# A retention and feed-forward kernel: each piece's outputs and the next piece's scores issued together

## The chip, the cores and the metric

One core of one Trainium2 chip runs the whole program. The metric is the device time in microseconds (us). Engines are named as in the profile: PE is TensorE's matmul, PEld its weight load (which overlaps matmuls), DVE is VectorE, ACT is ScalarE, POOL is GpSimd, SP is SyncE. SP does no arithmetic here; it issues nearly all DMA transfers, one after the other, from one queue.

## What is computed

A retention layer (8 batches, 8 heads, 576 positions, 64 dimensions a head), whose result is bridged to 4608 rows of 512 and fed through a feed-forward layer with 2048 hidden units:

```python
scores = scale * np.matmul(q, k.transpose(0, 1, 3, 2))
Dmat = np.where(rel >= 0, gamma[:, None, None] ** rel[None, :, :], 0.0)
attn_out = np.matmul(scores * Dmat[None], v)
x = attn_out.transpose(0, 2, 1, 3).reshape(4608, 512)
h = x @ w_in                                            # 512 x 2048
sp = np.maximum(h, 0.0) + np.log1p(np.exp(-np.abs(h)))
out = (h * erf(sp)) @ w_out                             # 2048 x 512
```

All inputs and outputs are float32; the weights arrive as 64-bit words and are rounded on the chip.

## The kernel before, in words

**Retention, by pieces.** The 4608 rows are cut into 36 pieces of 128 rows, numbered 0 to 35. Every ninth piece (8, 17, 26, 35) holds two half pieces of 64 rows, the tails of two batches. Retention runs in chunks within a batch: a piece needs its own scores and a running state that the piece before it left. A piece goes through three stages:

- `transposes(i)`, called T(i) below: queries and keys are brought into transposed form. For queries from piece 8 on and keys from piece 12 on this is done by DVE (L326) out of tiles `raw_qs` and `raw_ks`, which the DMA delivered in 32-row squares; for earlier pieces by TensorE (L332) and ACT. At its end T(i) calls `load(i + 2, "q")`, which puts the loads of the queries, and from piece 12 on of the keys, of piece i+2 into SP's queue (L131, four issues each for a full piece, eight for a pair of half pieces). `raw_qs` and `raw_ks` have two buffers each, so that load has to wait until T(i) has read its own.
- `scores(i)`, S(i): sixteen weight loads and matmuls on TensorE (L347) into two PSUM banks, then two DVE multiplications by a mask into `sT` (L352, seen as L99 in the profile, the line of the helper `tt`).
- `outputs(i)`, O(i): TensorE multiplies `sT` by the values (L365), adds keys times values for the state (L377) and the old state times the queries (L388); DVE then makes `sums` and two parts of `x` from it, POOL the new state (L426). At its end O(i) calls `load(i + 3, "kv")` (L147) and has POOL weigh the next piece's values (L313).

The list `stages` has them in the order T(i+1), O(i), S(i+1), for i from 0 on. `done[0]` is how many have been issued, and `attend(upto)` issues stages until `upto`. DVE, ACT, POOL and SP each carry out their instructions in the order in which the program issues them.

**Feed-forward, by products.** The rows are also cut into 9 chunks of 512 (four pieces each), the hidden units into 4 groups; the 36 pairs (group, chunk) are the blocks. Each of the two matrix products of a block is done in seven products in place of eight, with sums of sub-matrices, by the classes `First` and `Second`. One product is eight matmuls of 128x256 on TensorE in the profile (L496 for `First`, L604 for `Second`), some 1.7 us. In the order of issue within a block they are

`B11 B21 S4 A22 T2 T3 T1 A11 A12 B22 T4 S2 S3 S1`

where B and T belong to `Second` of a block and A and S (S1 to S4) to `First` of the next blocks. (S with a number of 5 or more, and S in general in the text, is the stage `scores`; products are named S1 to S4 only in this list and where a text says so.) Products accumulate in four PSUM banks: two that alternate (`ps_a`), one named e and one named g (`ps_e`, one buffer each). ACT copies the first partial results away, DVE adds the others: after A22 DVE adds bank g to `t` (`t<-g` in the profile), after which bank g is free for T3; T4's result is added to `o` (`o<-g`), after which g is free for S3. The first two chunks of group 0 are done as plain products (L550).

**How the two are woven.** `run(steps)` goes through a generator of products, and after each product calls `attend` for one more stage; the middle part of `Second` does the same in its own loop. So while pieces remain, TensorE sees three products for each piece, and between them T, O and S, one behind each product. `most[0]` bars the stages of chunks that may not begin yet, and is raised block by block; where the next block needs a chunk that is not finished, `attend(after_chunk(n + 2))` issues what is missing at once. The prologue has an order written out by hand (L754), with stages "a", products "p" and others. All pieces are finished about a third of the way through; the rest are products alone.

The weights are rounded in steps (`round_weights`: ACT L254 and L255, DVE L259, L263, L267, L272, POOL L274 and L275), and in the first third these steps stand between the stages too. Other DMA traffic in SP's queue: `xd<-x` stores a chunk of x for the later groups (L465, 1 MB), `od<-o` stores sums of outputs (L709, 512 KB each), `wraw` loads weights (L237).

Of the kernel before, what the change touches and what calls it, by code (L numbers as in the profile page):

```python
# [54 lines left out]
def kernel(  # L55
# [176 lines left out]
    def load_weights():  # L232
        part = next(coming, None)
        if part is not None:
            t = wraw.tile([P, 2 * WP], UINT32, tag="wraw", name="wraw")
            for rows, src in part[0]:
                nc.sync.dma_start(out=t[rows].rearrange("p (h f) -> p h f", h=2), in_=src)  # L237
            words.append((t, *part[1:]))
# [49 lines left out]
    def round_weights(n=1):  # L288
        for _ in range(n):
            next(round_step, None)  # L290
# [143 lines left out]
    stages = [(transposes, 0), (scores, 0)]  # L434
# [4 lines left out]
    stages = [(of, i) for of, i in stages if i < len(pieces)]  # L439
    done = [0]  # L440

    def before_chunk(c):

        return stages.index((outputs, c * PC)) if c < n_ch else len(stages)

    def after_chunk(c):

        return stages.index((outputs, (c + 1) * PC - 1)) + 1

    def attend(upto):  # L450
        while done[0] < min(upto, len(stages)):
            of, i = stages[done[0]]
            of(i)
            done[0] += 1
# [5 lines left out]
    def load_x(g, c):  # L460
        x[g, c] = x_tile()
        nc.sync.dma_start(out=x[g, c][:, :n_dc], in_=xd[c])
# [6 lines left out]
    def operands_x(g, c):  # L469
        summed.add((g, c))  # L470
        t = x[g, c]
        b11, b12, b21, b22 = (t[:, 2 * d : 2 * d + 2, h * TH : (h + 1) * TH] for d in range(2) for h in range(2))
        t1, t2, t4 = (t[:, n_dc + j, :].rearrange("p (d i) -> p d i", d=2) for j in range(3))
        if g == 0 or c < PLAIN:
            tt(t1, b12, b11, ALU.subtract)
            tt(t2, b22, t1, ALU.subtract)
            tt(b12, b22, b12, ALU.subtract)
        else:
            tt(t2, b12, b11, ALU.add)
            tt(t1, b22, t2, ALU.subtract)  # L480
        if g == 0:
            store_x(c)
        tt(t4, b21, t2, ALU.subtract)
        x[g, c] = {A11: b11, A12: b21, S4: b22, A22: t4, S1: t1, S2: t2, S3: b12}
# [254 lines left out]

    most = [before_chunk(2)]  # L740

    def run(steps, rounds=(), stages=1):

        for step, _ in enumerate(steps):
            attend(min(done[0] + stages, most[0]))
            round_weights(rounds[step] if step < len(rounds) else 0)

    keep_busy(10)
# [5 lines left out]
    for what in "alkakakawkakakawwaa3awa2aaa5ppppaa5wwppa5ppawappwcppa5ppaaapp5s":  # L754
        if what == "a":
            attend(done[0] + 1)
        elif what == "p":
            next(products)
        elif what == "s":
            store_x(0)  # L760
        elif what == "l":
            load(2, "kv")
        elif what == "c":
            nc.sync.dma_start(out=cst[:, CONST_FIRST:], in_=consts[:, CONST_FIRST:])
        elif what == "w":
            load_weights()
        elif what == "k":
            keep_busy(2)
        else:
            round_weights(int(what))  # L770
    most[0] = before_chunk(3)
    attend(after_chunk(1))
    store_x(1)
    for step, _ in enumerate(firsts[1].plain()):
# [8 lines left out]
        elif step == 8:  # L783
            firsts[0].sums()
    seconds[0].begin()
    run(seconds[0].first(), (2, 2))
    firsts[1].softplus()
    most[0] = before_chunk(4)
    for b, nxt in zip(blocks[2:], blocks[3:] + [None]):
        n = order.index((b.g, b.c))  # L790
        if isinstance(b, First):
            most_g[0] = order[n - 1][0] + 1
            run(b.middle(), (1, 1) if n != 2 else ())
            firsts[n - 1].sums()
            run(seconds[n - 1].first(), (1, 1) if n > 2 else ())
            run(b.last(), (1,) if 2 < n < n_ch else ())
            if n in (2, 3):
                load_weights()
            most[0] = before_chunk(n + 3)
        elif n + 2 < n_s:  # L800
            f = firsts[n + 1]
            for step, _ in enumerate(b.middle()):
                attend(min(done[0] + 1, most[0]))
                if step == 0:
                    f.erf()
                elif step == 1 and (n + 2 >= n_ch or done[0] == len(stages)):
                    operands_x(*order[n + 2])
                elif step == 2 and n_ch - 4 < n < n_ch:
                    round_weights()
            if order[n + 2] not in summed:  # L810
                attend(after_chunk(n + 2))
                operands_x(*order[n + 2])
            run(nxt.first(), (1,) if n > 1 else ())
            f.multiply()
            seconds[n + 1].begin()
            if n_ch <= n + 3 < n_s:
                load_x(*order[n + 3])
            run(b.last(), (0, 1) if n > 1 else ())
        elif n + 1 < n_s:
            firsts[n + 1].erf()  # L820
            seconds[n + 1].begin()
            rest = b.rest()
            for _ in range(3):
                next(rest)
            firsts[n + 1].multiply()
            run(rest)
            firsts[n + 1].sums((0,))
            steps = nxt.final()
            next(steps)
            firsts[n + 1].sums((1,))  # L830
            next(steps)
        else:
            run(steps)
# [30 lines left out]
```

## Time and profile before

Four runs gave 1025.52, 1026.39, 1026.18 and 1025.04 us, median 1025.85.

| what | value |
|---|---|
| profiled execution: its time | 1025.52 us |
| its span, first to last instruction | 1023.7 us |
| granted clock of TensorE | 1.00 throughout |
| DVE busy | 668.0 us of the span |
| ACT busy | 390.0 us |
| POOL busy | 122.1 us |
| DMA | 165.76 MB, mean 162 GB/s |
| share of the 16 DMA engines taken by SP's queue | 56.6% |
| first product of a block (L604) | at 83.8 us |
| last retention stage on TensorE (O35) | 311.6 to 313.4 us |

The time by 40 slices shows the two parts: the DMA engines are near full in the first twelve slices (25.6 us each), and half full afterwards; DVE is busier in the first part too. How to read what follows: a line in order of time has the start in us from the first instruction, the busy time in us, the engine, the line of the program, the operation, out<-in, the shape, how many instructions were merged, and in brackets the idle time of that engine just before, with what ended it. "issue" there means that nothing the profile shows was waited for. A stretch (from:to) has the busy time and number of instructions of PE, PEld, DVE, ACT and POOL, the granted clock, the share of the DMA engines that was busy, and GB/s.

### The profile page before, as it was taken

How to read it: one execution, taken by the hardware profiler on the slowest of the kernel's cores; microseconds unless marked ns; L12 is line 12 of the kernel's file. 1: busy time of each engine (PE TensorE's matmuls, PEld its weight loads, DVE VectorE, ACT ScalarE, POOL GpSimd, SP SyncE). 2: the span in 40 equal slices, each digit the busy share in tenths (PEclk: the TensorE clock that was granted, in tenths of full speed). 3: DMA queues.
4: the chain of work that ended last, by engine and by line, in shares of the span. 5: the costliest groups of instructions: out<-in, count | busy, mean ns of one | idle time of the engine just before them, and what ended most of it. 6: DMA issues, size and time to landing. Idle time of an engine off the chain costs nothing.

```text
span 1023.7 us, 15955 instructions
## 1 busy us (share of the span) xinstructions
PE 1014.6 (99%) x6348; PEld 878.3 (86%) x6348; DVE 668.0 (65%) x1062; ACT 390.0 (38%) x481; POOL 122.1 (12%) x122
## 2 busy tenths in 40 slices
PE   9999999999999999999999999999999999999998
PEld 8778888888788888888888888888888888888887
DVE  3769777967976656656666666666567655555555
ACT  2254133234135444334343444444433333333332
POOL 2143112122312010010001001000100000000000
PEclk9999999999999999999999999999999999999999
DMA  9998989979984354544445345434433333444434
GB/s 198 200 234 185 232 192 230 252 152 253 240 190 166 106 163 145 164 158 155 164 139 167 124 147 163 164 144 144 144 124 124 124 131 126 132 136 131 126 85 121
DMA packets 146986, 165.76 MB, mean 162 GB/s; under 512 B 97376, under 2 KB 121568, under 8 KB 138848
## 3 DMA queue, kind: packets, MB, share of 16 engines
q1 hardware_dynamic: 144832, 163.57, 56.6%
q10 hardware_dynamic: 2080, 1.18, 0.5%
q8 instruction: 50, 0.82, 0.3%
q14 instruction: 24, 0.20, 0.1%
HBM read 117.52 MB, written 47.19 MB: 161 GB/s over the span
## 4 chain that ended last, share of the span: by engine, by line
PE 89%; DMA 6%; SPq 2%; DVE 2%; issue 1%; POOL 0%; ACT 0%; ACTq 0%; DVEq 0%; POOLq 0%
PE a L604 23%; PE a L496 22%; PE g L496 11%; PE g L604 11%; PE e L604 6%; PE e L496 5%; PE o L365 3%; PE s L347 2%; DMA raw_v<-in_v_dram 2%; DMA raw_k<-in_k_dram 1%; DMA raw_ks<-in_k_dram 1%; PE o L388 1%; SPq L147 1%; PE o L377 1%; PE p L550 1%; PE f L668 1%
## 5 line engine op out<-in xcount | busy, mean ns | idle before, releaser
L496 PE MATMUL a<-x,wa 128*128 128x256 f32 x1088 | 258.3, 380 | 0.0
L496 PEld LDWEIGHTS a<-x,wa 128*128 128x128 f32 x1088 | 206.1, 190 | 28.6 <-issue 0.7
L604 PE MATMUL a<-wb,s 128*128 128x256 f32 x840 | 200.1, 381 | 0.0
L604 PEld LDWEIGHTS a<-wb,s 128*128 128x128 f32 x840 | 158.6, 190 | 23.0 <-ACT o L618 0.7
L99 DVE TENSOR_TENSOR t<-g,t 128x512 f32<-128x512 f32 x68 | 47.0, 691 | 150.2 <-ACT t L526 112.7
L496 PE MATMUL g<-x,wa 128*128 128x256 f32 x544 | 129.3, 381 | 0.0
L496 PEld LDWEIGHTS g<-x,wa 128*128 128x128 f32 x544 | 102.9, 190 | 14.4 <-issue 0.2
L99 DVE TENSOR_TENSOR o<-a,o 128x512 f32<-128x512 f32 x104 | 71.6, 688 | 46.4 <-PE a L604 46.4
L521 ACT COPY t<-a 128x512 f32<-128x512 f32 x34 | 19.9, 586 | 188.1 <-PE a L496 188.1
L99 DVE TENSOR_TENSOR t<-t,s 128x1024 f32<-128x1024 f32 x72 | 88.6, 1272 | 0.0
L565 ACT ACTIVATE s<-t 128x1024 f32<-128x1024 f32 x72 | 72.1, 1048 | 27.9 <-DVE t L99 27.9
L274 POOL TENSOR_TENSOR wraw<-wraw 128x512 f32<-128x512 f32 x28 | 29.4, 1051 | 436.5 <-DVE wraw L272 184.6
L99 DVE TENSOR_TENSOR x<-x 128x512 f32<-128x512 f32 x115 | 75.7, 692 | 1.2
L532 ACT COPY t<-a 128x512 f32<-128x512 f32 x34 | 19.9, 586 | 144.0 <-PE a L496 144.0
L569 ACT ACTIVATE s<-s 128x1024 f32<-128x1024 f32 x72 | 72.1, 1048 | 0.4
L604 PE MATMUL g<-wb,s 128*128 128x256 f32 x280 | 66.7, 381 | 0.0
L604 PE MATMUL a<-wb,t 128*128 128x256 f32 x280 | 66.6, 381 | 0.0
L604 PE MATMUL e<-wb,t 128*128 128x256 f32 x280 | 66.6, 381 | 0.0
L604 PE MATMUL g<-wb,t 128*128 128x256 f32 x280 | 66.4, 380 | 0.0
L496 PE MATMUL e<-x,wa 128*128 128x256 f32 x272 | 64.8, 381 | 0.0
L99 DVE TENSOR_TENSOR sT<-s,cst 128x512 f32<-128x512 f32 x72 | 46.2, 682 | 25.7 <-PE s L347 25.6
L99 DVE TENSOR_TENSOR o<-g,o 128x512 f32<-128x512 f32 x70 | 48.0, 685 | 21.4 <-ACT o L618 18.7
(86 smaller groups left out, 1248.5 us busy)
## 6 DMA issues: line engine op xcount, KB each, us to landing
od<-o SPq DMA_DIRECT2D x54, 512.0 KB, 3.3
x<-xd SPq DMA_DIRECT2D x27, 1024.0 KB, 4.8
o<-od SPq DMA_DIRECT2D x27, 1024.0 KB, 5.7
raw_qs<-in_q_dram SPq DMA_DIRECT2D x96, 112.0 KB, 4.5
raw_ks<-in_k_dram SPq DMA_DIRECT2D x84, 112.0 KB, 4.0
xd<-x SPq DMA_DIRECT2D x9, 1024.0 KB, 5.5
raw_v<-in_v_dram SPq DMA_DIRECT2D x64, 128.0 KB, 4.5
wraw<-in_moe_w_in_dram SPq DMA_DIRECT2D x32, 256.0 KB, 6.4
```

Of the source, the lines that this page charges most:

```text
L99: nc.vector.tensor_tensor(out=out, in0=in0, in1=in1, op=op)
L147: queue.dma_start(out=t[r0 : r0 + n, e::2, :], in_=heads.rearrange("h p d -> p h d"))
L274: engine.tensor_tensor(out=r_f, in0=high_f, in1=r_f, op=ALU.mult)
L347: nc.tensor.matmul(ps[e][:, p, :], lhsT=t["kT"][heads[e], p, :], rhs=t["qT"][heads[e], p, :], start=True, stop=True)
L365: nc.tensor.matmul(o[p % 2][heads[(e + p) % 2], p // 2, :], lhsT=t["v"][:, 2 * p + e, :], rhs=t["sT"][:, e, p, :], start=(p < 2), stop=(no ...
L377: nc.tensor.matmul(kv[heads[e], p, :], lhsT=t["k"][:, 2 * p + e, :], rhs=t["v"][:, 2 * p + e, :], start=False, stop=(p == NP - 1), skip_gr ...
L496: nc.tensor.matmul(acc[:, j * TH : (j + 1) * TH], lhsT=weights["wa", self.g][:, a, d, j * P : (j + 1) * P], rhs=x[self.g, self.c][a][:, d, :],
L521: nc.scalar.copy(out=self.t1[:, 1], in_=self.a)
L532: nc.scalar.copy(out=self.t2[:, 0], in_=self.a)
L565: nc.scalar.activation(self.s[:, j], t, AF.Softplus)
L569: nc.scalar.activation(self.s[:, j], self.s[:, j], AF.Erf)
L604: nc.tensor.matmul(acc[:, tp, :], lhsT=left[:, j * TH + tp * P : j * TH + (tp + 1) * P], rhs=weights["wb", self.g][:, b, j, :], start=(sta ...
```

## The change

A new function `attend_next` stands in for `attend` in the two loops that weave. When the next stage is an O, it does nothing the first time it is called, and at the second call issues O and at once the stage behind it, which is S of the next piece. A T is issued as before, behind one product. The parameter `stages` of `run`, always 1, is dropped.

```diff
+    held = [False]
+
+    def attend_next(upto):
+
+        if done[0] < upto and stages[done[0]][0] is outputs:
+            held[0] = not held[0]
+            if held[0]:
+                return
+            attend(done[0] + 1)
+        attend(min(done[0] + 1, upto))
+
     def attend(upto):
         while done[0] < min(upto, len(stages)):
             of, i = stages[done[0]]
...
-    def run(steps, rounds=(), stages=1):
+    def run(steps, rounds=()):
 
         for step, _ in enumerate(steps):
-            attend(min(done[0] + stages, most[0]))
+            attend_next(most[0])
             round_weights(rounds[step] if step < len(rounds) else 0)
...
             for step, _ in enumerate(b.middle()):
-                attend(min(done[0] + 1, most[0]))
+                attend_next(most[0])
                 if step == 0:
                     f.erf()
```

So for each piece TensorE sees, before: product, T, product, O, product, S (where T is DVE's work from piece 12 on); and after: product, T, product, product, O, S. The prologue, written out by hand, and the plain products of the second chunk call `attend` as before. Lines behind the new function stand 11 lines lower in the changed kernel.

## The prediction

> **What bounds the kernel now.** I read the page first: how busy the engines are, and the chain of work that ended last.
>
> ```profile
> PE 1014.6 (99%) x6348; PEld 878.3 (86%) x6348; DVE 668.0 (65%) x1062; ACT 390.0 (38%) x481; POOL 122.1 (12%) x122
> ...
> PE 89%; DMA 6%; SPq 2%; DVE 2%; issue 1%; POOL 0%; ACT 0%; ACTq 0%; DVEq 0%; POOLq 0%
> ```
>
> TensorE holds 89% of the chain, so the change, which only moves work, can pay in two ways: less idle time between TensorE's own instructions, or fewer waits. The small print of TensorE is best seen in its weight loads, in order of time (start, busy us, instruction, and in brackets the idle time before it). Retention next to the feed-forward products, in mid-stage:
>
> ```profile
> 165.14 0.85 PEld L365 LDWEIGHTS o<-sT,raw_v 128*64 128x64 f32 x16 [0.33 <-issue]
> ...
> 167.22 1.59 PEld L496 LDWEIGHTS g<-x,wa 128*128 128x128 f32 x8 [0.17 <-issue]
> 169.15 0.97 PEld L347 LDWEIGHTS s<-qT,kT 64*128 64x128 f32 x16 [0.33 <-issue]
> 170.24 1.59 PEld L604 LDWEIGHTS a<-wb,s 128*128 128x128 f32 x8
> ```
>
> Products alone, after the last piece:
>
> ```profile
> 314.97 1.70 PEld L604 LDWEIGHTS a<-wb,t 128*128 128x128 f32 x8
> 316.69 1.70 PEld L604 LDWEIGHTS e<-wb,t 128*128 128x128 f32 x8
> 318.42 1.70 PEld L496 LDWEIGHTS a<-x,wa 128*128 128x128 f32 x8
> ```
>
> A product among products takes 1.73 us from start to start. The one squeezed between O and S takes 169.15 - 167.22 = 1.93. That is the whole tax which the change can remove. Does it come back between O and S, when they touch? The prologue has one such place:
>
> ```profile
> 53.96 0.42 PEld L388 LDWEIGHTS o<-qT,state 64*64 64x64 f32 x16
> 54.56 0.97 PEld L347 LDWEIGHTS s<-qT,kT 64*128 64x128 f32 x16 [0.17 <-issue]
> 55.65 0.73 PEld L550 LDWEIGHTS pe<-x,wa 128*128 128x128 f32 x4
> ```
>
> O there starts at 52.48 and takes 2.08 until S starts, as the O at 165.14 takes 2.08 until a product starts; S takes 1.09 in both. It does not come back.
>
> **Step 1, TensorE's own time.** In the order of the built program S follows O directly for pieces 11 and 13 to 35: 24 places (S12 stays apart, because O11 is called for at once before the operands of chunk 2). Nothing else is removed or added: every matmul, DVE, ACT and POOL instruction and every DMA is there again. 24 x (1.93 - 1.73) = 4.8 us, if nothing else waits. Bounds: 0 to 4.8 from this step alone.
>
> The Trainium skill speaks against it: "TensorEngine Tiling (Array Packing)", Key Properties, says that a change of tiling mode drains TensorE, and O (64x64) to S (64x128) is such a change. By the rule that change would cost the 0.33 that S pays behind a product, not the 0.17 of the row at 54.56; 0.04 would be left of each 0.20, 1.0 us in all. The row decides.
>
> **Step 2, the loads.** The queries and keys of a piece come by SP's queue. A load for piece i+2 is issued behind T(i), whose buffer it takes. The queue in order of time:
>
> ```profile
> 119.81 0.93 SPq L147 DMA_DIRECT2D raw_k<-in_k_dram  x2
> 120.84 1.00 SPq L147 DMA_DIRECT2D raw_v<-in_v_dram  x2
> 123.46 3.84 SPq L131 DMA_DIRECT2D raw_qs<-in_q_dram  x8
> ```
>
> Before 123.46 SP waits 1.6 us, for T15. From load 18 on, up to 303, each load starts 2.7 to 14 us behind the T that freed its buffer, so T gates none of them: SP issues without pause at 0.43 us each, or is held up by transfers. Stretches of 6 us (the last two columns are the DMA share and GB/s) show the two by turns:
>
> ```profile
> 126.00:132.00 6.00, 6.00 (x51) 4.86 (x51) 3.67 (x5) 3.60 (x4) 1.05 (x2) 1.00 0.48 105
> 144.00:150.00 6.00, 6.00 (x68) 5.02 (x72) 5.92 (x8) 0.59 (x1) 2.97 (x3) 1.00 1.20 221
> 210.00:216.00 6.00, 6.00 (x77) 5.05 (x77) 2.60 (x7) 5.19 (x6) 1.61 (x2) 1.00 0.42 91
> 222.00:228.00 6.00, 6.00 (x45) 4.81 (x45) 5.70 (x10) 0.58 (x1) 1.81 (x2) 1.00 0.96 190
> ```
>
> Where the share is near 1 the transfers are the limit, and where it is half (sixteen small issues for a half piece) the issuing is. Either way a faster TensorE does not hurry it. So the loads keep their pace, and only their start moves. How much? The previous gate is T13 (SP waits 2.2 us before 106.05), one pair (S11) into the change: 0.2 earlier, so the load ahead of 123.46 ends at 121.84 - 0.2 = 121.64. T15 itself is no gate any more: in the changed order the four sums of 0.69 us ahead of it on DVE (120.20 to 122.8) stand behind it, and S14 is 0.6 earlier. Load 17 starts at about 121.65, 1.8 us sooner. Bounds: 0.6 (the three pairs S11, S13, S14 alone) and the full gain of TensorE at that place (3.6 at piece 29).
>
> **Step 3, the new wait.** DVE runs its list in order, so an instruction behind a transpose waits for that transpose's load. Before, where T29 falls:
>
> ```profile
> 245.91 0.71 DVE L326 STREAM_TRANSPOSE qT<-raw_qs 128x512 f32<-128x512 f32 x1 [1.46 <-DMA raw_qs<-in_q_dram]
> 247.04 1.12 DVE L326 STREAM_TRANSPOSE kT<-raw_ks 128x512 f32<-128x512 f32 x1 [0.41 <-DMA raw_ks<-in_k_dram]
> 247.99 0.43 DVE L263 TENSOR_SCALAR wa<-wa 128x512 uint32<-128x512 uint32 x1
> 248.45 0.69 DVE L267 SCALAR_TENSOR_TENSOR wa<-wraw,wa 128x512 uint32<-128x512 uint32 x1
> 249.06 0.68 DVE L99 TENSOR_TENSOR t<-g,t 128x512 f32<-128x512 f32 x1
> ```
>
> ```profile
> 249.94 1.59 PEld L604 LDWEIGHTS g<-wb,s 128*128 128x128 f32 x8 [0.17 <-DVE t L99]
> ```
>
> T29 waits for its load, the addition t<-g (it empties bank g after A22) waits behind T29, and T3 needs bank g: already 0.17 late. Before, O28 ran between T2 and T3 and filled most of that time. Now the order is A22, T2, T3, O28, S29, so the filler stands behind the waiting product. Shifted by step 2, T3 can start at 249.94 - 1.8 = 248.1; then T3 2.03 (a product ahead of O, as from 163.11 to 165.14), O 2.09, S 1.09: S29 ends at 253.35, against 252.96 before. So 18 pairs (3.6 us) have been swallowed, and 0.4 is lost. The same triple stands at T25 and T33. At T25 the load comes sooner still, since in the changed list a 1 MB store of x stands behind load 24 and one 512 KB store of o behind load 25, both ahead of it before; at T33 the addition ends at 286.79, so T3 is possible at 287.0 - 1.8 = 285.2.
>
> From 253.35 to S31: T1 1.62 (a product behind S, as from 170.24), A11 1.73, A12 2.03, O29 2.09, S30 1.09, B22 1.62, T4 1.73, S2 2.03, O30 2.09 = 16.03, so S31 starts at 269.4. Before it was 270.7, with 1.06 us of waiting for kT behind DVE (two multiplications that took 3.50) and 0.24 inside O30; TensorE, coming later, now meets that work finished, or at most about 0.2 later. Ahead by 1.3. S32: 278.85 - 1.3 - 0.2; its end, four products (1.62 and three of 1.73) later, is 285.25, so T33 no longer holds anything. Three more pairs, S33 to S35: ahead by 2.1 in the end. What else moves costs nothing: O has a product more between S and itself, so sT (1.28) is ready sooner; a piece's x is due a product later but still two products ahead of its use; the K and V loads behind O wait in a queue that is itself that late. Without that lag they would be 1.7 us later.
>
> **The sum** stands against the profiled execution: 1023.7 span, 1025.52 with what lies around it, 0.33 below the median 1025.85 of the runs shown. 1025.52 - 2.1 = 1023.4; as a median, 1023.75. I give 1023.7. From 0.2%, 2.05 us, on, a difference is more than the measurement leaves open, so the forecast lies on that line.
>
> **Rivals.** (a) The loads follow TensorE and nothing waits: 4.8 off, 1021.05. For it: DMA is at half share twice in the stretch, and many loads landed 5 us ahead of their S. Against: T25 and T27 to T30 waited for loads, and S27 started 0.15 us after kT. (b) The loads start only 0.6 earlier: S29 ends at 254.55, S31 gains what it can, 0.9 in the end, 1024.95. For it: DMA share is 1.01 at 120 to 126, so an issue 1.2 us sooner may only queue. (c) Slower: load 29 lands later, because loads and stores stand differently in the queue. The price is one for one through T3: time = 1023.75 + delay. It overtakes the old time when the last keys of piece 29 land 0.3 after the old 246.91, and leaves 0.2% at 249.3. Two stores of 512 KB in front, at 248 GB/s, are 4.2 us: 1027.95. Against it: in the built order the same stores stand ahead of load 29 as before. That the pairs do not form is excluded by the built order.
>
> **Numbers.** Forecast 0.42 (own range 1022.5 to 1024.9), (a) 0.20, (b) 0.20, (c) 0.18. Six in ten of the forecast lies beyond 0.2%: faster 0.42 x 0.6 + 0.20 = 0.45; same 0.17 + 0.20 + 0.01 = 0.38; slower 0.17. The range takes in (a) and (b) and the lower part of (c): 1020.9 to 1027.0.
>
> **What would show it.** Right: S behind O with 0.17 idle at 24 places, 1.73 for the product that was between; T3 after T29 waiting some 2.5 us for DVE's t<-g; load 17 issued near 121.7; S31 without its 1.06. Wrong: no wait at T3 and loads landing 3 us earlier near 245 (a); loads as before (b); a landing of keys 29 after 247.2 (c); or idle time at O to S above 0.33.

## The result, and the profile after

The changed kernel takes 1028.04 us (median of 43 runs, 1024.08 to 1032.25) against 1026.06 for the kernel before (63 runs, 1023.44 to 1031.35): a ratio of 1.0018, 95% interval [1.0012, 1.0024]. It is slower by 0.18%, about 2 us, where 1023.7 was forecast. The profiled execution took 1026.0, span 1024.2, at a mean granted clock of 0.998.

The page's busy times, and the shares of the chain that ended last:

```profile
PE 1010.8 (99%) x6348; PEld 879.9 (86%) x6348; DVE 663.8 (65%) x1062; ACT 390.0 (38%) x481; POOL 119.8 (12%) x122
...
PE 87%; DMA 7%; SPq 3%; DVE 2%; issue 1%; POOL 0%; ACT 0%; DVEq 0%; POOLq 0%
```

TensorE is busy for 3.8 us less than before, and the span is 0.5 longer: what was saved has become idle time. In the chain TensorE has given two points to DMA and to SP's queue.

**The pairs** stand as forecast (weight loads of the changed kernel, in order of time, the counterpart of the stretch at 165.14 before):

```profile
163.36 0.85 PEld L365 LDWEIGHTS o<-sT,raw_v 128*64 128x64 f32 x16 [0.33 <-issue]
...
165.45 0.97 PEld L347 LDWEIGHTS s<-qT,kT 64*128 64x128 f32 x16 [0.17 <-issue]
166.54 1.59 PEld L507 LDWEIGHTS g<-x,wa 128*128 128x128 f32 x8
168.16 1.70 PEld L615 LDWEIGHTS a<-wb,s 128*128 128x128 f32 x8
169.88 1.70 PEld L615 LDWEIGHTS g<-wb,s 128*128 128x128 f32 x8
```

O to S is 2.09, S to product 1.09, the product behind S 1.62 and the next 1.72: the 1.93 between O and S is gone. Of the drain that a change of tiling mode would bring, no more than these 0.17 us of idle time between O and S can be seen.

**The loads** (SP's queue in order of time):

```profile
120.53 1.87 SPq L147 DMA_DIRECT2D raw_v<-in_v_dram  x2
122.50 4.54 SPq L131 DMA_DIRECT2D raw_qs<-in_q_dram  x8
127.14 3.71 SPq L131 DMA_DIRECT2D raw_ks<-in_k_dram  x8
130.96 3.52 SPq L147 DMA_DIRECT2D raw_v<-in_v_dram  x4
134.58 1.50 SPq L131 DMA_DIRECT2D raw_qs<-in_q_dram  x3
```

Load 17 starts at 122.50, not at 121.65: the two issues of values ahead of it took 1.87 instead of 1.00. Its own first eight take 4.54 instead of 3.84, so load 18 starts at 134.58, where before it started at 134.77. Of a head start of 1.8 us, 0.2 is left. The keys of piece 29 land at 248.05 (before: 246.91); DVE's transpose of them starts at 248.18.

**Where TensorE stands still.** First the product T3 of the block at T25, on PE, and what it waits for, on DVE:

```profile
206.31 1.89 PE L615 MATMUL a<-wb,s 128*128 128x256 f32 x8
210.35 1.99 PE L615 MATMUL g<-wb,s 128*128 128x256 f32 x8 [2.15 <-DVE t L99]
```

```profile
208.36 1.09 DVE L326 STREAM_TRANSPOSE kT<-raw_ks 128x512 f32<-128x512 f32 x1 [1.13 <-DMA raw_ks<-in_k_dram]
209.30 0.41 DVE L259 TENSOR_SCALAR wa<-wa 128x512 f32<-128x512 f32 x1
209.63 0.67 DVE L99 TENSOR_TENSOR t<-g,t 128x512 f32<-128x512 f32 x1
```

Step 3's new wait stands there as it was described, but at T25, where the forecast expected the load sooner. At T29, where the forecast had T3 wait some 2.5 us, it hardly waits (weight loads, then DVE):

```profile
248.58 1.70 PEld L615 LDWEIGHTS a<-wb,s 128*128 128x128 f32 x8
250.93 1.59 PEld L615 LDWEIGHTS g<-wb,s 128*128 128x128 f32 x8 [0.64 <-DVE t L99]
```

```profile
248.18 1.11 DVE L326 STREAM_TRANSPOSE kT<-raw_ks 128x512 f32<-128x512 f32 x1 [0.79 <-DMA raw_ks<-in_k_dram]
250.19 0.69 DVE L99 TENSOR_TENSOR t<-g,t 128x512 f32<-128x512 f32 x1
```

TensorE came there late itself. One reason lies between the two places, at the scores S27 (weight loads), which wait for keys directly:

```profile
230.63 0.33 PEld L388 LDWEIGHTS o<-qT,state 64*64 64x64 f32 x16
232.82 1.71 PEld L347 LDWEIGHTS s<-qT,kT 64*128 64x128 f32 x16 [1.85 <-issue]
234.75 2.40 PEld L507 LDWEIGHTS g<-x,wa 128*128 128x128 f32 x8 [0.22 <-DVE x L99]
237.17 1.70 PEld L507 LDWEIGHTS a<-x,wa 128*128 128x128 f32 x8
```

After that wait S27 takes 1.93 from start to start instead of 1.09, and the product behind it 2.42 instead of 1.62. Stretches, with the busy time of PE first and the granted clock third from the end, show why:

```profile
229.59:233.00 3.41, 1.67 (x50) 1.38 (x48) 2.09 (x3) 1.63 (x3) 0.00 (x0) 1.00 0.87 199
233.00:236.42 3.42, 3.42 (x20) 2.93 (x21) 3.10 (x8) 0.00 (x0) 1.04 (x1) 0.50 1.09 241
```

Behind a stretch of 3.41 us in which TensorE was idle for 1.74, it is granted half its clock for the next 3.41. No row of the kernel before shows this in its profiled execution. In 44 runs of the changed kernel the mean clock was below 1.0 in 36 (median 1028.31 us), and 1.0 in 8 (median 1025.98, the time of the kernel before). Of 126 runs of the kernel before, taken beside the experiments, 103 had 1.0 (median 1026.33 us); the other 23 were no slower (1026.34).

So two theories to test. A: the loads take the whole gain of the pairs, and the idle waits which this makes bring drops of the clock on top. B: the pairs, or the T3 that lost its filler, cost what they save. All ratios below are to the kernel before, run beside each.

### The profile page after: what moved, and what is told of

The parts are those of the page before. It is cut to its first block, busy times and chain, and to the rows that moved or that the text cites. A ratio compares the mean times of both kernels' runs of the same rounds, so it can differ in the third digit from the quotient of the medians.

```text
span 1024.2 us, 15959 instructions
## 1 busy us (share of the span) xinstructions
PE 1010.8 (99%) x6348; PEld 879.9 (86%) x6348; DVE 663.8 (65%) x1062; ACT 390.0 (38%) x481; POOL 119.8 (12%) x122
## 4 chain that ended last, share of the span: by engine, by line
PE 87%; DMA 7%; SPq 3%; DVE 2%; issue 1%; POOL 0%; ACT 0%; DVEq 0%; POOLq 0%
PE a L615 22%; PE a L507 22%; PE g L615 11%; PE g L507 11%; PE e L615 6%; PE e L507 5%; PE s L347 2%; PE o L365 2%; DMA raw_k<-in_k_dram 2%; DMA raw_ks<-in_k_dram 1%; DMA raw_qs<-in_q_dram 1%; SPq L131 1%; DMA wraw<-in_moe_w_in_dram 1%; SPq L147 1%; PE o L388 1%; DMA raw_v<-in_v_dram 1%
## 5 line engine op out<-in xcount | busy, mean ns | idle before, releaser
L615 PEld LDWEIGHTS g<-wb,s 128*128 128x128 f32 x280 | 52.9, 190 | 10.5 <-DVE t L99 3.2
```

Of the source, the lines that this page charges most:

```text
L615: nc.tensor.matmul(acc[:, tp, :], lhsT=left[:, j * TH + tp * P : j * TH + (tp + 1) * P], rhs=weights["wb", self.g][:, b, j, :], start=(sta ...
```

## Experiments on the loads and the pairs

**Fewer loads.** Both kernels without the row loads of the keys of full pieces from 12 on. The state product of these pieces takes the values in their place, so TensorE's work stays and the result is another one:

```diff
-                elif name == "v" or i < SQUARES_K or len(pieces[i]) == 1:
+                elif name == "v" or i < SQUARES_K:
...
-                        lhsT=t["k"][:, 2 * p + e, :],
+                        lhsT=t.get("k", t["v"])[:, 2 * p + e, :],
```

> The kernel before, with the row loads of the keys left out for full pieces from piece 12 on: 256 KB of some 1408 KB a piece; the state product of those pieces takes values in place of keys, so that part of the computation is changed and its time kept. It is the base for the next kernel. Theory A (loads set the pace only from piece 17 on, and before the change they bind little): 1021 to 1025 us, the waits for keys of about 1.06 us at S31 gone. Theory B (loads do not bind anywhere): within 0.5 us of the kernel before.

> The changed kernel with the same loads left out (row loads of the keys for full pieces from piece 12 on; the state product takes values in place of keys). Theory A (the 24 pairs each gain 0.2 us on TensorE, and loads swallow it): with the loads out of the way it is 3 to 5 us faster than the kernel before with the same loads left out, no wait over 0.5 us stands at S27 or T3, and the granted clock stays 1.0 from 100 to 310 us. Theory B (the pair itself costs what it gains, by its place among VectorE's and ScalarE's work): within 1 us of that kernel, or slower.

Measured: 1024.05 without the change (ratio 0.9975 [0.9966, 0.9985]) and 1018.33 with it (0.9922 [0.9910, 0.9934]). With less to load the same edit is worth 5.7 us (A had 3 to 5) instead of -2. The changed order now runs like this (stretches of the second kernel):

```profile
200.00:225.00 25.00, 25.00 (x215) 21.59 (x214) 17.66 (x32) 9.39 (x11) 7.72 (x9) 1.00 0.86 184
225.00:250.00 25.00, 25.00 (x251) 21.38 (x250) 19.05 (x34) 10.54 (x13) 4.95 (x5) 1.00 0.94 215
```

PE is never idle, the clock is full; in neither kernel does the profile show a wait of PE between 100 and 320 us. The spans are 1022.1 and 1016.9, 5.2 apart; 0.7 of that is there at S12 already (100.89 and 100.16), before all but one of the pairs. The other 4.5 are the 4.8 of step 1, nearly. A holds; B falls for the pairs.

**Only late pairs, only early pairs.**

```diff
-        if done[0] < upto and stages[done[0]][0] is outputs:
+        if done[0] < upto and stages[done[0]][0] is outputs and stages[done[0]][1] >= 30:
```

> The order of before up to the scores S30; pairs (outputs with the next scores directly behind) from the outputs O30 on, five of the 24. Theory A (a pair saves 0.2 us of TensorE's time wherever no load binds, and in the stretch before S31 the loads take it all): time 0.6 to 1.2 us below the kernel before, ratio 0.9988 to 0.9995, the granted clock 1.0. Theory B (a pair costs what it saves): ratio 0.9998 or more.

> The changed kernel with the pairs up to the outputs O29 only, and from O30 on the order of before (the counterpart of e5_late). Theory A (19 of the 24 pairs lie in the stretch where loads take their gain and the idle waits bring dips of the clock; the five late ones gain 0.7 us): ratio to the kernel before 1.0015 to 1.0035, the clock below 1.0 in most runs. Theory B (the late pairs are what costs): ratio 1.0005 or less.

Late pairs alone: 1025.66, ratio 0.9993 [0.9985, 1.0002]; the profiled run keeps clock 1.0, and from S31 (271.03) to S35 (308.51) it takes 37.48, before 37.86, where four pairs should give 0.8. The median fits A, but the interval includes 1. Early pairs alone (the same condition with `< 30`): 1028.94, ratio 1.0026 [1.0015, 1.0038]. This decides more: all that slows the change down lies in the 19 pairs before S31, where loads set the pace.

**The filler back between T2 and T3.**

```diff
-    def attend_next(upto):
+    def attend_next(upto, hold=True):
...
-            held[0] = not held[0]
+            held[0] = hold and not held[0]
...
-                attend_next(most[0])
+                attend_next(most[0], hold=step > 0 or n not in (3, 4, 5))
```

> The changed kernel, but in the three blocks with a second multiplication of chunks whose product T3 stood waiting (T3 at 210.4, 250.9 and 288.0 us) the outputs and scores are put back between T2 and T3, where the kernel before has them; elsewhere the pairs stay. Theory A (the loads of keys and values keep their own pace, and TensorE can only choose where it waits): the stalls of T2 (2.5, 0.6 and 0.1 us) go, but the scores S27 still wait for keys that land at about 231.5 us, and S29 for its own; the stage S31 starts within 0.6 us of the changed kernel's 272.05, and the time is 0 to 1 us below it (ratio to the kernel before between 1.0008 and 1.0020). Theory B (the product T3 moved away from its filler is the whole loss): the 3.2 us of those stalls come back, the ratio to the kernel before is below 0.9995.

1027.39, ratio 1.0012 [1.0003, 1.0021]. What PE waited for between 100 and 320 us (total, times, longest), in the changed kernel and then in this one:

```profile
PE s L347 <- DVE kT L326: 2.5, 3, 1.7
PE g L615 <- DVE t L99: 2.4, 2, 2.2
```

```profile
PE s L347 <- DVE kT L326: 5.7, 3, 3.5
```

The waits at T3 are gone, and S26 and S27 wait that much longer. S29 starts at 254.76 (changed kernel: 254.94). That is A: TensorE can choose only where it waits. B falls for T3 too. The clock was below 1.0 in all 11 runs.

**SP's issuing.** The values of the half pieces 17 and 26 from ACT's queue, in the changed kernel and in the one before:

```diff
-                queue = nc.scalar if (name, i) == ("k", 0) else nc.sync
+                queue = nc.scalar if (name, i) == ("k", 0) or name == "v" and i in (17, 26) else nc.sync
```

> The changed kernel, with the four row loads of the values of each of the half pieces 17 and 26 issued on ScalarE's queue instead of SP's (3.4 us of SP's time at 131.0 to 134.5, the like at 217.9 to 222). Theory A (SP's time for issuing is what keeps the loads behind the half pieces, while the DMA share is 0.71 to 0.76 there): load 18 begins near 131.5 instead of 134.6, loads 18 to 29 land 2 to 4 us earlier, S27 waits less than 0.5 us, and the time falls to a ratio of 0.9965 to 0.9990. Theory B (the transfers themselves are full, or ScalarE's copies are held back by the issues): loads 27 to 29 land within 1 us of the changed kernel's, ratio 1.0005 or more.

> The kernel before with the same eight issues on ScalarE's queue, as the base for the kernel above. Theory A: its only waits for loads (0.4 to 1.06 us around S27, S30 and S31) go, ratio 0.9985 to 0.9998, so that the pairs are worth 2 us or more once the loads come earlier. Theory B: ratio 0.9998 to 1.0010.

1026.57, ratio 0.9993 [0.9983, 1.0002], and 1025.35, ratio 0.9986 [0.9978, 0.9995]. My mechanism failed for the changed kernel: load 18 started at 134.33, not 131.5, since the issues of load 17 on SP now took until 134.2. And ACT, which carries out its list in order, was held up (ACT in order of time):

```profile
208.01 3.54 ACTq L147 DMA_DIRECT2D raw_v<-in_v_dram  x4
211.59 0.66 ACT L254 ACTIVATE wa<-wraw 128x512 f32<-128x512 f32 x1 [13.21 <-DMA raw_v<-in_v_dram]
```

DVE's `wa<-wa` waited for that activation, behind it t<-g, and T3 waited 5.3 us. The Trainium skill ("DMA: Bandwidth & Descriptors", Rules for kernel authors) says that spreading transfers over issuing engines adds no bandwidth and only saves issue time. Load 18 starts no earlier, so not even issue time was saved here; and since the DMA share was 0.53 from 126 to 132 us, where the issues of load 17 grew from 3.71 to 5.00 us, full transfers don't explain it. The kernel before fits A: its wait at S31 falls from 1.0 to 0.2 us, and S12 to S35 takes 206.90 us in its profile instead of 207.80. Why the changed kernel with these issues has a ratio of 0.9993 instead of 1.0018, though its profile shows so long a wait and its clock was below 1.0 in 10 of 11 runs, stays open.

## Experiments on the clock

**Filling the idle time with idle work.** Matmuls of 128x128 into PSUM columns that nothing reads, behind O(26) in the changed kernel; then behind O(25) and O(26) in the kernel with the filler back:

```diff
+        for _ in range(8 if i == 26 else 0):
+            nc.tensor.matmul(flat(o[1])[:, 2 * P : 3 * P], lhsT=ones, rhs=ones, start=False, stop=True, skip_group_check=True)
...
+        for _ in range({25: 6, 26: 13}.get(i, 0)):
```

> The changed kernel with 8 more products of 128x128 behind the outputs of piece 26, written into columns of PSUM that nothing reads, about 1.8 us of TensorE's time at the place where S27 waited 1.75 us and the granted clock then fell to 0.5 for 3.4 us. Theory A (the idle wait brings the half clock, and it costs 1.6 us over the stretch): no entry below 1.0 between 225 and 260 us, S27 starts at 232.8 as before and takes 1.1 us instead of 1.93, and the time is 1 to 2 us below the changed kernel's, ratio to the kernel before 0.9995 to 1.0010. Theory B (the clock dip comes from something else, or is made up at the next late load): the time is that of the changed kernel or up to 1.8 us more, ratio 1.0015 to 1.0035.

> The kernel of e1_filler (outputs and scores back between T2 and T3) with 6 more products of 128x128 behind the outputs of piece 25 and 13 behind those of piece 26, into columns of PSUM that nothing reads, about 1.5 and 3.2 us, so that the two long waits of that kernel (1.55 us at S26, 3.58 us at S27) are filled with work. Theory A (the loads set where S27 starts, and the idle waits add the dips of the clock, which cost 2 us or more in a run): the clock is 1.0 in most runs instead of 0.997 to 0.998 in all 11, S27 starts within 0.8 us of 232.0, and the ratio to the kernel before falls from 1.0012 to 0.9985 to 1.0002. Theory B (the dips cost nothing of weight): ratio 1.0008 to 1.0025.

The first was inconclusive: 1027.56, ratio 1.0012 [1.0002, 1.0021]. S27 ran at full clock and took 1.09, but in that execution T3 waited longer, and the half clock came there, at 210.87. Five of its 12 runs had a clock of 1.0, and their median of 1027.35 is hardly below the 1027.77 of the others.

The second decides for its own kernel: 1025.69, ratio 0.9992 [0.9984, 1.0001], against 1.0012 [1.0003, 1.0021] without the idle matmuls, and the clock was 1.0 in 11 of 12 runs (0.999 in the other) where it had been 0.997 or 0.998 in all 11. TensorE does 19 matmuls more and the kernel is about 2 us faster. The starts of S27 and S28 (PE), without the idle matmuls and then with them:

```profile
232.05 2.08 PE L347 MATMUL s<-qT,kT 64*128 64x128 f32 x16 [3.54 <-DVE kT L326]
242.75 1.16 PE L347 MATMUL s<-qT,kT 64*128 64x128 f32 x16
```

```profile
232.82 1.16 PE L347 MATMUL s<-qT,kT 64*128 64x128 f32 x16 [1.27 <-DVE kT L326]
240.78 1.16 PE L347 MATMUL s<-qT,kT 64*128 64x128 f32 x16
```

The same work takes 10.70 us behind the long wait and 7.96 at full clock. S27 starts 0.8 later than without the idle matmuls, and S29, at 252.78, 2.0 earlier. So in the kernel with the filler back the drops of the clock cost about 2 us.

For the changed kernel that is not shown. Its runs at full clock are 2.3 us faster than its others, but a run whose loads come sooner has fewer waits as well as fewer drops. In its profiled execution the drop behind S27 took 1.6 us (0.84 in S27, 0.80 in the product), and a later wait made it up: T3 at T29 could not start before t<-g ended, at 250.88.

The kernel with early pairs shows an execution with two drops, each behind a long wait at T3:

```profile
208.12:211.53 3.41, 0.51 (x2) 0.49 (x3) 2.28 (x4) 0.53 (x1) 0.19 (x1) 1.00 0.94 231
211.53:214.94 3.41, 3.41 (x13) 2.35 (x14) 0.00 (x0) 3.38 (x5) 0.00 (x0) 0.50 0.42 89
249.08:252.49 3.41, 1.30 (x7) 0.80 (x5) 2.85 (x5) 0.00 (x0) 0.00 (x0) 1.00 1.03 250
252.49:255.90 3.41, 2.86 (x7) 2.32 (x8) 0.49 (x1) 2.86 (x4) 0.00 (x0) 0.50 1.00 267
```

Up to S29 its order is that of the changed kernel, whose profiled execution had one drop. S29 starts here at 258.45, there at 254.94, 3.5 earlier. The second of these waits, on PE:

```profile
253.04 3.39 PE L615 MATMUL g<-wb,s 128*128 128x256 f32 x8 [2.66 <-DVE t L99]
256.36 1.09 PE L365 MATMUL o<-sT,raw_v 128*64 128x128 f32 x16
```

The keys of piece 29 land at 250.19, 2.1 later than in the changed kernel's profile, and T3 starts 2.1 later. T3 then takes 3.32 until O28 starts, against 1.92 there: 1.4 from the half clock. The first drop was made up by this wait. So 2.1 of the 3.5 us are later keys and 1.4 the clock. Why the keys land later in this execution is open, and no profile shows an execution of the changed kernel near its median.

## Experiments on the path of a late load

If TensorE must wait at S26 and S27, products could be drawn into the wait. Behind S28 five stand in a row. Two kernels with the filler back hold O(25) and O(26) for one product more each, or O(26) for two:

```diff
+    later = [25, 26]
...
         if done[0] < upto and stages[done[0]][0] is outputs:
+            if stages[done[0]][1] in later:
+                later.remove(stages[done[0]][1])
+                return
```

> The kernel of e1_filler with the outputs of pieces 25 and 26 one product later each: two products that stood in a row of five behind S28 are drawn ahead, one in front of O25 and one in front of O26, where TensorE waited 1.55 us (S26) and 3.58 us (S27) for keys. No work is added or left out. Theory A (the loads set where S26 and S27 start, TensorE's idle time there is the loss, and the dips come on top): S27 starts at 232 +/- 1 as in e1_filler, S29 some 3.2 us earlier (251.0 to 252.0 instead of 254.76), dips fewer than in e1_filler, ratio to the kernel before 0.9955 to 0.9985. Theory B (the loads follow what TensorE does, so that a later piece only makes later loads): S29 no earlier than 254, ratio 0.9995 or more.

> As e9_shift, with the outputs of piece 26 one product later still (three products drawn ahead in all, two stay behind S28). Theory A: S27 no longer waits, or under 0.5 us; S29 starts when its own keys allow it (249.4 to 250.5), the clock is 1.0 in most runs, ratio to the kernel before between that of e9_shift and 0.0020 below it. Theory B: S28 and S29 turn late in their place, ratio at or above that of e9_shift.

Misses: 1027.35, ratio 1.0008 [0.9997, 1.0018], and 1027.75, ratio 1.0012 [1.0004, 1.0021]; S29 at 255.70 and 255.63. Those are B's numbers, but not by B's cause: the keys of piece 29 had landed at 248.38 and 249.00, some 7 us before. The second kernel's profile shows the cause, first PE, then DVE:

```profile
226.35 1.89 PE L511 MATMUL a<-x,wa 128*128 128x256 f32 x8
233.99 3.54 PE L511 MATMUL g<-x,wa 128*128 128x256 f32 x8 [5.75 <-DVE o L99]
```

```profile
232.33 1.09 DVE L326 STREAM_TRANSPOSE kT<-raw_ks 128x512 f32<-128x512 f32 x1 [1.66 <-DMA raw_ks<-in_k_dram]
233.27 0.67 DVE L99 TENSOR_TENSOR o<-g,o 128x512 f32<-128x512 f32 x1
```

The product drawn ahead needs bank g, and o<-g, which empties it, stands behind the transposes of piece 27 in DVE's list. It needs no load, and waits for one all the same. So the transposes have to move too:

```diff
+        if done[0] < upto and stages[done[0]][0] is transposes and stages[done[0]][1] in later:
+            later.remove(stages[done[0]][1])
+            return
```

with `later` as [26, 27], [26, 27, 27] and [24, 26, 27], and [26, 27] in the kernel before.

> The order of TensorE as in e9_shift (two products drawn ahead of O25 and O26), but the transposes of pieces 26 and 27 stand one product later on VectorE too, so that what frees the PSUM tile g (the sum o<-g, which in e10_shift3 waited behind the transposes of piece 27 until 233.3 us and held a product of TensorE for 5.75 us) comes ahead of the wait for the load. Theory A (it is VectorE's order that passes the wait for a load on to products that need no load): no product waits for VectorE's o<-g or t<-g over 1 us between 205 and 260 us, S29 starts between 250.5 and 252.5, at most one entry of the half clock, ratio to the kernel before 0.9955 to 0.9990. Theory B (the loads fall back by as much as the transposes do): loads 28 and 29 land 1.5 us or more later than in e1_filler, ratio 0.9998 or more.

> As e12_later_t with the transposes of piece 27 two products later (three products drawn ahead in all). Theory A: S27 does not wait over 0.5 us, S29 starts as its own keys allow, 249.4 to 251.5, clock 1.0 in most runs, ratio 0.9945 to 0.9985. Theory B: as above, ratio 0.9998 or more.

> As e12_later_t, and the transposes of piece 24 one product later as well (drawn from the same row of five behind S28). Theory A: the wait of 0.7 us at S24 goes, S29 and the time as in e13_later_t3 within 1 us. Theory B: ratio 0.9998 or more.

> The kernel before with the transposes, outputs and scores of pieces 26 and 27 one product later each, without pairs: what the shift alone is worth. Theory A: the kernel before waits little for loads ahead of S29 (0.3 us at S27), so the shift alone gives 0 to 0.7 us, ratio 0.9990 to 1.0003. Theory B (the shift does all, the pairs nothing): ratio within 0.0007 of that of e12_later_t.

| kernel | median us | ratio, 95% | S29 starts |
|---|---|---|---|
| [26, 27] | 1025.88 | 0.9993 [0.9985, 1.0002] | 250.12 |
| [26, 27, 27] | 1024.49 | 0.9986 [0.9975, 0.9997] | 251.12 |
| [24, 26, 27] | 1024.73 | 0.9985 [0.9974, 0.9996] | 251.69 |
| before, [26, 27] | 1025.20 | 0.9991 [0.9982, 0.9999] | 252.54 |

S29 starts 4.0 to 5.6 us earlier than with the outputs moved alone, so DVE's order was the path, as A has it. A's ratios were a little too hopeful for the first two, and some waits remain: for o<-g 1.9 us in the first, 1.4 in the second, 2.7 in the third. The clock was 1.0 in 2 of 12, 4 of 12 and 4 of 11 runs, where A had it in most for the second. The second and third kernels are faster than both kernels of this case. The shift alone, without pairs, gives 0.9991, inside A's bounds and B's. The intervals overlap, so how much of the 0.9985 the pairs add is not settled.

## Why the prediction was wrong, by its steps

- **Step 1 (4.8 us of TensorE's time): right.** O to S costs 0.17 idle, the product between falls to 1.72, and with fewer loads some 4.5 of the 4.8 arrive.
- **Step 2, "Load 17 starts at about 121.65, 1.8 us sooner": this step failed.** I read that the loads keep their pace, and then let their start move by the time at which SP's wait for T15 ends. But the transfers were full there (DMA share 1.01 at 120 to 126 before, 1.02 after), and SP's issues of the values and of load 17's first half took 1.6 us longer: earlier issues only queued, which fits rival (b). With 0.2 of the head start left at load 18, the keys of pieces 18 to 28 landed from 0.9 sooner to 2.2 later than before, and those of piece 29 1.1 later, where the forecast needs them 1.8 sooner. The same stores stand ahead of load 29 in both kernels; what moved the loads between 18 and 29 is not shown. Keys at 248.05 are the case that rival (c) priced (slower once they land after 247.2), though no store was added.
- **Step 3's wait: right in kind, wrong in place.** Its 2.5 us stand not at T29 (0.64 there) but at T25 (2.15), and S27's direct wait of 1.75 is in no sum. So T3 at T29, forecast for 248.1, was held from two sides: t<-g ended at 250.88, and TensorE, one product of 1.73 behind the weight loads at 248.58, was itself ready only at 250.3, since the waits and the half clock had taken more than the pairs had saved. With the keys on time T3 would still have been about 2.2 late.
- **The rest of the sum: right, from a wrong start.** T3 started at 250.93, 2.8 late; from there to the end of S29 5.10 us (forecast 5.21); from there to S31 16.02 (forecast 16.03). Against before, the kernel is 1.35 behind at S31 and 0.56 at S35: the late pairs give the 0.8 that was forecast. The profiled execution is 2.6 above the 1023.4 forecast for it, and the 2.8 at T3 account for that. That two delays which the sum did not have ended there within 0.6 us of each other is luck.
- **T25 was judged wrongly.** "At T25 the load comes sooner still": the stores stood as the forecast said, but the keys landed at 208.28 (before 208.60), only 0.3 sooner, while S24 had started 3.6 us sooner (199.93 and 203.56). T3 waited 2.15 there.
- **A term was missing.** No rival had a price for the slower clock behind idle time. With 2.8 more the forecast median is 1026.5; measured is 1028.04, beyond the range's upper end of 1027.0. In the slow execution that has a profile, of the kernel with early pairs, the loads land later still and the clock drops twice. How the other 1.5 us divide between the two is not shown for the changed kernel.

## What to carry to other kernels

Time saved on the bounding engine is worth something only where what feeds it can come earlier as well. A stretch whose inputs arrive at their own pace swallows it, and an earlier issue into full transfers is no earlier arrival. A late load stops not only the work that needs it, but all that stands behind its first reader in that engine's list. Hold that reader back, before drawing other work ahead. And a wait of TensorE can cost twice, once as idle time and once by the slower clock behind it, unless a later wait makes that up.

## What was not expected of the hardware

The half clock comes on a fixed grid. I cut the traces of all 17 kernels into steps of 3413 ns (the length of the shortest drops) from the first change of the clock on. From 20 us to the last products, all ten drops from full clock follow a step in which TensorE was idle for 1.75 us or more (1.75, 1.80, 2.09, 2.11, 2.11, 2.46, 2.90, 3.03, 3.40, 3.41). Of the steps with no drop behind them the idlest have 1.68, 1.64, 1.63 and 1.58, and one exception, in the prologue of the kernel before with ACT's queue (33.01 to 36.42), has 1.83. So the limit lies near half a step; the exception is not explained. The nearest pair, first the shifted kernel [24, 26, 27] with no drop behind it, then [26, 27, 27] with one at 252.74:

```profile
226.97:230.38 3.41, 1.74 (x9) 1.18 (x7) 3.41 (x4) 1.64 (x3) 2.10 (x1) 1.00 0.88 217
```

```profile
249.33:252.74 3.41, 1.62 (x18) 1.49 (x19) 2.48 (x5) 2.54 (x3) 0.61 (x1) 1.00 1.11 253
```

So a wait's place decides: at T3 in the changed kernel 2.15 us fell across two steps (0.91 and 1.24 idle in them) and cost nothing more, and at S27 1.75 us fell into one and halved the clock. That may be one reason why runs of one kernel differ; each kernel has one profile only, so it is not shown. The Trainium skill ("TensorE: Matmul & The Clock Gate", What's actually happening) has the free-running window of 3413 ns, which these traces agree with; its table puts the slow clock behind a whole idle window, where in these traces about half of one was enough.
